# Banded attention and a four-expert FFN on one core: values two steps behind scores in the opening, other times for the weights

## The chip, the cores and the metric

The kernel runs on one core of a Trainium2 chip. What counts is the device time of one execution in microseconds. The kernel before takes 850.36 us in the median of three runs (849.62 to 850.9).

## The reference, cut to what matters

```python
def attn(q, k, v):                      # B=4, H=8, S=576, D=64
    s = (q @ k.transpose(0, 1, 3, 2)) / sqrt(64)
    rel = pos[:, None] - pos[None, :]
    plain = (rel >= 0) & (rel < 32)                      # heads 0 to 3
    dil = (rel >= 0) & (rel < 128) & (rel % 4 == 0)      # heads 4 to 7
    s = where(mask, s, -1e9); s = s - s.max(-1)
    a = exp(s); a = a / (a.sum(-1) + 1e-9)
    return a @ v
def moe(x, probs, w1, w2):              # N=2304, D=512, E=4, F=1024
    p = probs / (probs.sum(-1) + 1e-9)
    return sum(p[:, e] * (relu(x @ w1[e]) @ w2[e]) for e in range(4))
out = moe(attn(q, k, v) as rows of 512, probs, w1, w2)
```

## The kernel before, in words

**The attention** is cut into 48 groups: a batch, a pair of heads and a third of the sequence. They go in 25 steps (`steps`, L628): the first two hold one group each, the others two. The stages of a step are scores on TensorE (`s_qk`, tile sc, L271), six row maxima on VectorE that also put the masked scores into SBUF (`s_max`, L285), a subtraction on GpSimdE (`s_sub`, L301), the exponential on ScalarE (`s_exp`, L309), row sum and reciprocal on VectorE (`s_sum`, L317 and L318), the normalisation on GpSimdE (`s_norm`, L325), three transposes on TensorE and their copy by ScalarE (`s_tr`, tiles pt and pts, L336 and L340), and the product with the values on TensorE (`s_av`, tile po, L356), which ScalarE copies into xr (L372), the FFN's input. The tiles sc, pt and po take turns in four PSUM banks (pool pa).

**The loop** is at L713. In turn n it issues loads of q and k on SyncE's queue and of v on ScalarE's (for batches 0 and 1), and then the stages in the order of a table: the number beside a stage says how many steps it is behind. In before scores are at 0, transposes at 3, products at 4. The order in which the program issues is the order on each engine.

**The FFN** runs on expert blocks u of 256 columns and blocks of 576 rows of x. fp32 is done as three products of a high and a low part (names ending in h and l), and the first layer by Strassen-like sums (tiles m1x, m1y, hidden rows hh and hl), the second layer into m and the accumulator acc. The high part is a copy on ScalarE (L117), the low part a subtraction on VectorE or GpSimdE (L120). Pieces that split and sum weights and x are generators in a list `queue`: `step()` does one of them (a filler), and `need(...)` does all that stand ahead of one that is needed now. From turn START on (10 in before), the loop also takes two pieces of FFN a turn; `next(ffn)` may answer "idle". From OPEN on (15) it takes PACE of them a turn, until attention is done. Turns without FFN hold dummy matmuls (tile wt, L685) and fillers.

`fetch_w1` and `fetch_w2` load weights on SyncE's queue, `w1_split`, `w1_sums`, `w1_late` and `w2_late` are the pieces that prepare them; pw are the experts' shares, loaded in turn 4 (L740) and normalised by `weigh`. `done(groups)` says in which turn the last of some groups has had its product, from which START, OPEN and the times of the x pieces (`when`) follow.

Of the kernel before, what the change touches and what calls it, by code (L numbers as in the profile page):

```python
# [8 lines left out]
F32 = mybir.dt.float32  # L9
# [4 lines left out]
WINDOW = 32  # L14
# [4 lines left out]
GB = 6  # L19
GS = GB // 2  # L20
GW = GB * QB
PACE = 12


def band_masks(S):


    import numpy as np

    masks, which = [], []  # L30
    for run in (S, S // DILATION):
        for i in range(S // SB):
            a = (i * SB + np.arange(SB))[:, None]
            c = a // QB * QB - WINDOW + np.arange(KB)[None, :]
            seen = (c >= 0) & (a - c >= 0) & (a - c < WINDOW) & (a // run == c // run)
            m = np.where(seen, np.float32(0), np.float32(-8e9))
            same = [j for j, other in enumerate(masks) if np.array_equal(other, m)]
            if not same:
                same = [len(masks)]
                masks.append(m)  # L40
            which.append(same[0])
    return np.stack(masks), which
# [3 lines left out]
def kernel(  # L46
# [11 lines left out]
    nc = tc.nc  # L58
    _, which = band_masks(qT.shape[3])
    B, NP, _, S = qT.shape  # L60
    GP = S // GW
    NT, DM = out.shape
    E, _, F = w1.shape
# [18 lines left out]
    pw = const.tile([128, NTT, E], F32, name="pw")  # L82
# [16 lines left out]
    def fetch_w1(u):  # L99
        e, s = divmod(u % NU, FPE)  # L100
        r = wp.tile([128, 4, FU], F32, tag="r1", name="r1", bufs=2)
        nc.sync.dma_start(
            out=r, in_=w1[e, :, s * FU:(s + 1) * FU].rearrange("(c p) f -> p c f", p=128)
        )
        raw1[u] = r

    def fetch_w2(u):
        e, s = divmod(u % NU, FPE)
        r = wp.tile([128, 2, DM], F32, tag="r2", name="r2")
        nc.sync.dma_start(  # L110
            out=r, in_=w2[e, s * FU:(s + 1) * FU, :].rearrange("(c p) d -> p c d", p=128)
        )
        raw2[u] = r
# [110 lines left out]
    def attention(ap, xrp, pa):  # L224
# [18 lines left out]
            nc.gpsimd.memset(t[:, :, KB:], 1e-9)  # L243

        def load_qk(b, p, gi):
            q_s = ap.tile([128, GW], F32, tag="q", name="q_s", bufs=6)
            k_s = ap.tile([128, GW + WINDOW], F32, tag="k", name="k_s", bufs=6)
            nc.sync.dma_start(out=q_s, in_=qT[b, p][:, gi * GW:(gi + 1) * GW])
            nc.sync.dma_start(out=k_s, in_=kT[b, p][:, gi * GW:(gi + 1) * GW + WINDOW])
            qk_t[b, p, gi] = (q_s, k_s)  # L250
# [123 lines left out]
        def load_masks():  # L374
            nc.sync.dma_start(out=mask, in_=masks)


        stages = (
            (s_sub, 1), (s_sum, 2), (s_av, 4), (s_tr, 3), (s_norm, 2), (s_exp, 1),
            (s_qk, 0), (s_max, 0),  # L380
        )
        return chunk, load_masks, load_qk, load_v, stages


# [191 lines left out]
    def step(of=None):  # L576
        of = queue if of is None else of
        while of:
            if next(of[0][1], 0) != 0:
                return  # L580
            of.pop(0)

    def prepare(what, *args, soon=False, of=None):
        of = queue if of is None else of
        of.insert(0 if soon else len(of), ((what, args), what(*args)))
# [11 lines left out]
    with tc.manual_schedule():  # L597
# [11 lines left out]
        ap = early.enter_context(tc.tile_pool(name="attn", bufs=2, side="right"))  # L609
        xr_pool = xrp.__enter__()  # L610

        pools["chunk"], load_masks, load_qk, load_v, stages = attention(ap, xr_pool, pa)
        pairs = [(b, p) for b in range(B) for p in range(NP)]
        h0, h1 = range(NP // 2), range(NP // 2, NP)

        def batch(b, thirds):

            g = [(b, p, i) for p in h0 for i in range(GP)]
            return g + [(b, p, i) for part in thirds for p in h1 for i in part]
# [3 lines left out]
        first = batch(0, ((0, 2), (1,)))  # L623
# [2 lines left out]
            rest += batch(b, (range(GP),))  # L626
        rest = first + rest
        steps = [rest[:1], rest[1:2]] + [rest[i:i + 2] for i in range(2, len(rest), 2)]  # L628
        LAG = 4

        def done(*gs):

            return LAG + max(n for n, s in enumerate(steps) if any(g in s for g in gs))

        def begin():

# [17 lines left out]
        def weigh():  # L654

            nc.vector.reduce_sum(out=ps_, in_=pw, axis=mybir.AxisListType.X)
            nc.vector.tensor_scalar(
                out=ps_, in0=ps_, scalar1=1e-9, scalar2=None, op0=ALU.add
            )
            nc.vector.reciprocal(out=pr_, in_=ps_)  # L660
            nc.vector.tensor_tensor(
                out=pn, in0=pw, in1=pr_.to_broadcast([128, NTT, E]), op=ALU.mult
            )
# [17 lines left out]
        def dummies(n):  # L681

            for _ in range(n):
                wt = pools["m2"].tile([128, 512], F32, tag="m2", name="wt")
                nc.tensor.matmul(wt[:, :256], warm[:, :128], warm, start=True, stop=True)  # L685
# [5 lines left out]
        def dil(b, *thirds):  # L691
            return plains[b] + [(b, p, i) for p in h1 for i in thirds]


        START = done(*dil(0, 0, 2)) + 1
        OPEN = done(*dil(1, 0)) + 1
        when = {}
        for n, i, names in (
            (done(*plains[0]), 0, ("B11",)), (done(*plains[0]), 1, ("B11",)),
            (START - 1, 0, ("B21",)), (START - 1, 1, ("B21",)),  # L700
            (done(*dil(0, 1)), 0, ("X12", "B22", None, "t2", "t1", "t3")),
            (OPEN - 1, 1, ("X12", "B22", None)),
            (done(*dil(1, 1, 2)), 2, X_PARTS), (done(*dil(2, 0, 1)), 3, X_PARTS),
        ):
            when.setdefault(n, []).append((i, names))

        flat = [g for s in steps for g in s]
        first_x = []
        qk_done = qk_next = v_next = 0

        dummies(18)
        ffn = experts(begin)
        for n in range(len(steps) + LAG):  # L713
            while qk_next < min(qk_done + min(6, 3 + n), len(flat)):
                load_qk(*flat[qk_next])
                if qk_next == 0:
                    load_masks()
                qk_next += 1
            while v_next < len(steps) and v_next < max(n - LAG, 0) + 3 and v_next <= n:
                load_v(v_next, steps[v_next])  # L720
                v_next += 1
            for stage, lag in stages:
                if 0 <= n - lag < len(steps):
                    stage(n - lag, steps[n - lag])
            if n < len(steps):
                qk_done += len(steps[n])
            for i, names in when.get(n, ()):
                for name in names:
                    of = first_x if i < 2 else later
                    if name is None or name == "T2":  # L730
                        prepare(x_sums, i, of=of)
                    if name is not None:
                        prepare(x_part, i, name.upper(), of=of)
            queue[:0] = first_x
            first_x.clear()
            if n == 3:
                fetch_w1(0)
            if n == 4:
                fetch_w2(0)
                nc.sync.dma_start(out=pw, in_=probs.rearrange("(t p) e -> p t e", p=128))  # L740
            if n == 5:
                prepare(w1_split, 0)
            if n == 7:
                prepare(w2_late, 0)
                fetch_w1(1)
            if n == START + 1:
                weigh()
                prepare(w1_split, 1)
                prepare(w1_sums, 1)
            if n == OPEN - 1:  # L750
                prepare(w2_late, 1)
            if n == START + 2:
                fetch_w2(1)
            if n == OPEN:
                fetch_w1(2)
            if n == OPEN:
                gate.add("open")
            if n < START:
                dummies(4 if n < 4 else 1)
                step()  # L760
                if n > 4:
                    step()
                    step()
                continue
            for _ in range(PACE if "open" in gate else 2):
                if next(ffn) == "idle":
                    dummies(2)
                    for _ in range(3):
                        step()
                    break  # L770
                step()
                if len(queue) > 8:
                    step()
                elif later and len(queue) < 5:
                    step(later)
# [61 lines left out]
```

## Time and profile before

| | before |
|---|---|
| median of 3 runs | 850.36 us |
| profiled execution | 853.5 us, span 851.5 us |
| TensorE busy | 830.2 us, 97% of the span |
| VectorE, GpSimdE, ScalarE busy | 482.9, 404.5, 319.4 us |

```profile
PE   8798899999999999999999999999999999999998
DVE  4565755668656568755555545555555555455554
POOL 3456977777677668931431432332341341242210
PEclk8589999999999999999999999999999999999999
DMA  8872334223231122310100100100101001010003
```

Each digit is a fortieth of the span, 21.3 us; 9 is 90% or more busy. PEclk is TensorE's granted clock in tenths of full speed, which is 2.4 GHz; the other level is 1.2 GHz. The attention's opening is in the first three slices, and the second of them has the low clock. The chain of work that ended last is TensorE's for 90% of the span.

### The profile page before, as it was taken

What the parts mean: (1) busy time and instruction counts of PE and PEld (TensorE: products, weight loads), DVE (VectorE), ACT (ScalarE), POOL (GpSimd) and SP (SyncE); (2) the same over time, 40 slices, a digit from 0 to 9 for tenths busy, and PEclk for the clock granted to TensorE, in tenths of its full rate; (3) what the DMA queues carried; (4) which work ended last, traced back from release to release, by engine and by line L of the source; (5) the groups of instructions that cost most, each with busy time, mean ns of one, the idle gap of its engine ahead of it and who ended that gap; (6) DMA issues with size and microseconds to landing.
All of it is one profiled execution on the core that took longest, in us unless ns stands there. A gap on an engine that the chain in (4) does not pass through costs nothing.

```text
span 851.5 us, 15556 instructions
## 1 busy us (share of the span) xinstructions
PE 830.2 (97%) x6173; PEld 733.4 (86%) x6173; DVE 482.9 (57%) x1015; ACT 319.4 (38%) x761; POOL 404.5 (48%) x484
## 2 busy tenths in 40 slices
PE   8798899999999999999999999999999999999998
PEld 5577788888888888889899898898898998988986
DVE  4565755668656568755555545555555555455554
ACT  2344454545444444533333233232242242232321
POOL 3456977777677668931431432332341341242210
PEclk8589999999999999999999999999999999999999
DMA  8872334223231122310100100100101001010003
GB/s 233 217 197 77 122 112 122 89 90 118 83 102 61 50 75 75 124 49 26 50 26 25 50 25 26 50 26 27 49 25 50 26 26 50 25 34 17 1 25 123
DMA packets 51463, 59.16 MB, mean 69 GB/s; under 512 B 5952, under 2 KB 40896, under 8 KB 51392
## 3 DMA queue, kind: packets, MB, share of 16 engines
q1 hardware_dynamic: 47936, 53.46, 20.0%
q10 hardware_dynamic: 3456, 4.72, 2.2%
q8 instruction: 48, 0.79, 0.4%
q14 instruction: 23, 0.19, 0.1%
HBM read 53.45 MB, written 4.72 MB: 68 GB/s over the span
## 4 chain that ended last, share of the span: by engine, by line
PE 90%; DVE 3%; ACT 2%; DMA 2%; POOL 1%; issue 1%; ACTq 0%; POOLq 0%; DVEq 0%
PE m L487 45%; PE m1x L389 23%; PE m1y L389 17%; PE po L356 2%; PE sc L271 2%; DMA q_s<-qT 1%; PE pt L336 1%; PE wt L685 1%; DVE hl L413 1%; DMA v_s<-vw 1%; DVE acc L495 1%; DVE xl_T L120 1%; POOL g1l L120 0%; ACT hh L407 0%; DVE xr L207 0%
## 5 line engine op out<-in xcount | busy, mean ns | idle before, releaser
L495 DVE SCALAR_TENSOR_TENSOR acc<-m,pn,acc 128x512 f32<-128x512 f32 x270 | 201.8, 749 | 133.0 <-PE m L487 132.8
L487 PE MATMUL m<-w2h,hh 128*128 128x512 f32 x576 | 227.3, 395 | 3.6 <-DVE acc L495 3.1
L487 PE MATMUL m<-w2l,hh 128*128 128x512 f32 x576 | 226.0, 392 | 0.0
L120 POOL TENSOR_TENSOR g2l<-r,g2h 128x256 fp32r<-128x256 f32 x124 | 93.0, 777 | 240.7 <-PE m L487 212.2
L487 PE MATMUL m<-w2h,hl 128*128 128x512 f32 x576 | 179.1, 392 | 0.1
L407 ACT ACTIVATE hh<-s 128x384 fp32r<-128x384 f32 x94 | 49.4, 526 | 248.3 <-DVE s L430 197.8
L487 PEld LDWEIGHTS m<-w2h,hh 128*128 128x128 f32 x576 | 108.3, 188 | 26.2 <-DVE acc L495 5.7
L487 PEld LDWEIGHTS m<-w2h,hl 128*128 128x128 f32 x576 | 108.3, 188 | 24.3 <-DVE hl L413 0.6
L487 PEld LDWEIGHTS m<-w2l,hh 128*128 128x128 f32 x576 | 108.5, 188 | 20.1
L120 POOL TENSOR_TENSOR g1l<-r,g1h 128x256 fp32r<-128x256 f32 x93 | 69.1, 759 | 72.0 <-ACT g1h L117 72.0
L120 POOL TENSOR_TENSOR w2l<-r,w2h 128x512 fp32r<-128x512 f32 x62 | 80.5, 1317 | 45.4 <-ACT w2h L117 45.0
L446 DVE TENSOR_TENSOR s<-m1x,s 128x384 f32<-128x384 f32 x47 | 26.2, 558 | 103.2 <-PE m1x L389 101.7
L439 ACT ACTIVATE u<-m1x 128x384 f32<-128x384 f32 x47 | 23.1, 491 | 145.9 <-PE m1x L389 145.9
L413 DVE SCALAR_TENSOR_TENSOR hl<-s,hh 128x384 fp32r<-128x384 f32 x94 | 61.0, 648 | 28.8 <-ACT hh L407 28.8
L389 PE MATMUL m1x<-xh_T,g2h 128*128 128x384 f32 x156 | 52.9, 339 | 2.1 <-DVE s L430 1.8
L389 PE MATMUL m1x<-xl_T,g2h 128*128 128x384 f32 x156 | 52.5, 336 | 0.0
L389 PE MATMUL m1x<-xh_T,g2l 128*128 128x384 f32 x156 | 52.3, 335 | 0.0
L117 ACT ACTIVATE g2h<-r 128x256 fp32r<-128x256 f32 x125 | 43.4, 405 | 3.9 <-POOL r L149 3.9
L285 DVE CUSTOM_DVE_ANT_0 sm<-sc,mask 128x64 f32<-128x64 f32 x144 | 23.0, 222 | 36.8 <-PE sc L271 36.1
L389 PE MATMUL m1y<-xl_B,g2h 128*128 128x384 f32 x128 | 43.4, 339 | 0.0
L389 PE MATMUL m1y<-xh_B,g2h 128*128 128x384 f32 x128 | 43.4, 339 | 0.0
L389 PE MATMUL m1y<-xh_B,g2l 128*128 128x384 f32 x128 | 43.3, 338 | 0.0
(91 smaller groups left out, 1507.6 us busy)
## 6 DMA issues: line engine op xcount, KB each, us to landing
r<-w SPq DMA_DIRECT2D x64, 512.0 KB, 3.4
k_s<-kT SPq DMA_DIRECT2D x48, 112.0 KB, 3.5
v_s<-vw ACTq DMA_DIRECT2D x24, 192.0 KB, 4.5
q_s<-qT SPq DMA_DIRECT2D x48, 96.0 KB, 3.9
v_s<-vw SPq DMA_DIRECT2D x24, 192.0 KB, 3.8
out<-acc SPq DMA_DIRECT2D x18, 256.0 KB, 2.0
mask<-masks SPq DMA_DIRECT2D x1, 192.0 KB, 4.1
pw<-probs SPq DMA_DIRECT2D x1, 36.0 KB
```

What stands on the lines that cost most here:

```text
L117: nc.scalar.activation(out=hi, in_=src, func=AF.Copy)
L120: lo_eng.tensor_tensor(out=lo, in0=src, in1=hi.bitcast(F32), op=ALU.subtract)
L271: nc.tensor.matmul(banks[swap][o:o + QB, i * KB:(i + 1) * KB], q_s[h, c0:c0 + QB], k_s[h, c0:c0 + KB], start=True, stop=True, skip_group_c ...
L285: nc.vector.tensor_tensor_reduce(out=sm[:, i * len(gs) + k, :KB], in0=banks[k][:, i * KB:(i + 1) * KB], in1=mask[:, which[blk if p < NP // ...
L356: nc.tensor.matmul(po[k][64 * j:64 * j + 64, o:o + QB], v_s[rows, j, 2 * i + half, :], ts_[rows, c:c + QB], start=True, stop=True,)
L389: nc.tensor.matmul(bank, w[:, k], x[:, k], start=(first and k == 0 and i == 0), stop=(last and k == 1 and i == 2), skip_group_check=True,)
L407: nc.scalar.activation(out=hi, in_=src, func=AF.Relu)
L413: nc.vector.scalar_tensor_tensor(out=lo, in0=src, scalar=0.0, in1=hi.bitcast(F32), op0=ALU.max, op1=ALU.subtract)
L439: nc.scalar.activation(out=u2, in_=x, func=AF.Copy)
L446: nc.vector.tensor_tensor(out=s5, in0=x, in1=s5, op=ALU.add)
L487: nc.tensor.matmul(po, h, w, start=(n == 0 and x == 0), stop=(n == 3))
L495: nc.vector.scalar_tensor_tensor(out=acc, in0=po, scalar=pn[:, tt, e:e + 1], in1=acc, op0=ALU.mult, op1=ALU.add,)
```

## The change

Steps 0 to 10 (those up to the group `(1, NP - 1, 0)`, `opening` in number) get a table of their own, `first`: products two steps behind scores, transposes one, and another order of issue. With `done` it moves START from 10 to 8 and OPEN from 15 to 13. Turn numbers of loads and splits are now told from START: first weights in turn 4 (3 before), w2 in turn 6 (4), `w1_split(0)` in turn 6 (5), `w2_late(0)` in turn 8 (7), the second weights and `weigh` in turn 7 (7 and 11), their split and sums in turn 9 (11). pw is the very first transfer, on ScalarE's queue. At most four groups of q and k are loaded ahead, in four buffers each. Turns ahead of START hold four fillers and two dummies (four in the first three turns); a turn that is idle four fillers. PACE is 10.

```diff
-PACE = 12
+PACE = 10
...
-            q_s = ap.tile([128, GW], F32, tag="q", name="q_s", bufs=6)
-            k_s = ap.tile([128, GW + WINDOW], F32, tag="k", name="k_s", bufs=6)
+            q_s = ap.tile([128, GW], F32, tag="q", name="q_s", bufs=4)
+            k_s = ap.tile([128, GW + WINDOW], F32, tag="k", name="k_s", bufs=4)
...
-        stages = (
+        first = (
+            (s_sum, 1), (s_norm, 1), (s_av, 2), (s_qk, 0), (s_max, 0), (s_tr, 1),
+            (s_sub, 0), (s_exp, 0),
+        )
+        then = (
             (s_sub, 1), (s_sum, 2), (s_av, 4), (s_tr, 3), (s_norm, 2), (s_exp, 1),
             (s_qk, 0), (s_max, 0),
         )
+        stages = (first, then)
...
-        LAG = 4
+        AHEAD = 4
+        opening = [n for n, s in enumerate(steps) if (1, NP - 1, 0) in s][0] + 1
+
+        def lag(n):
+
+            return 2 if n < opening else 4
 
         def done(*gs):
 
-            return LAG + max(n for n, s in enumerate(steps) if any(g in s for g in gs))
+            return max(n + lag(n) for n, s in enumerate(steps) if any(g in s for g in gs))
...
+        nc.scalar.dma_start(out=pw, in_=probs.rearrange("(t p) e -> p t e", p=128))
         dummies(18)
         ffn = experts(begin)
-        for n in range(len(steps) + LAG):
-            while qk_next < min(qk_done + min(6, 3 + n), len(flat)):
+        for n in range(len(steps) + 4):
+            while qk_next < min(qk_done + AHEAD, len(flat)):
...
-            while v_next < len(steps) and v_next < max(n - LAG, 0) + 3 and v_next <= n:
+            while v_next < len(steps) and v_next + lag(v_next) <= n + 2:
                 load_v(v_next, steps[v_next])
                 v_next += 1
-            for stage, lag in stages:
-                if 0 <= n - lag < len(steps):
-                    stage(n - lag, steps[n - lag])
+            for late, order in enumerate(stages):
+                for stage, after in order:
+                    if 0 <= n - after < len(steps) and late == (n - after >= opening):
+                        stage(n - after, steps[n - after])
...
-            if n == 3:
+            if n == START - 4:
                 fetch_w1(0)
-            if n == 4:
+            if n == START - 2:
                 fetch_w2(0)
-                nc.sync.dma_start(out=pw, in_=probs.rearrange("(t p) e -> p t e", p=128))
-            if n == 5:
                 prepare(w1_split, 0)
-            if n == 7:
+            if n == START - 1:
+                fetch_w1(1)
+                weigh()
+            if n == START:
                 prepare(w2_late, 0)
-                fetch_w1(1)
             if n == START + 1:
-                weigh()
                 prepare(w1_split, 1)
                 prepare(w1_sums, 1)
+            if n == START + 2:
+                fetch_w2(1)
             if n == OPEN - 1:
                 prepare(w2_late, 1)
-            if n == START + 2:
-                fetch_w2(1)
...
             if n < START:
-                dummies(4 if n < 4 else 1)
-                step()
-                if n > 4:
-                    step()
+                dummies(4 if n < 3 else 2)
+                for _ in range(4):
                     step()
                 continue
             for _ in range(PACE if "open" in gate else 2):
                 if next(ffn) == "idle":
                     dummies(2)
-                    for _ in range(3):
+                    for _ in range(4):
                         step()
```

The order on TensorE just ahead of the first expert product, before (po is the product with values, pt the transposes, sc the scores, wt a dummy, m1x the first FFN product):

```order
L356 MATMUL po<-pts,v_s 64x32 x24
L336 MATMUL pt<-ident,pb 128x128 x3
L271 MATMUL sc<-k_s,q_s 32x64 x24
L685 LDWEIGHTS ident
L685 MATMUL wt<-ident 128x256
L356 MATMUL po<-pts,v_s 64x32 x24
L336 MATMUL pt<-ident,pb 128x128 x3
L271 MATMUL sc<-k_s,q_s 32x64 x24
L389 MATMUL m1x<-xh_B_0_681,g1h 128x384
```

And the same place in the changed kernel:

```order
L695 LDWEIGHTS ident
L695 MATMUL wt<-ident 128x256
L695 LDWEIGHTS ident
L695 MATMUL wt<-ident 128x256
L356 MATMUL po<-pts,v_s 64x32 x24
L271 MATMUL sc<-k_s,q_s 32x64 x24
L336 MATMUL pt<-ident,pb 128x128 x3
L394 MATMUL m1x<-xh_B_0_563,g1h 128x384
```

The transposes have moved behind the scores, and there they belong to the step before these scores and not to the one three steps back; two dummies stand between them and the next product.

The order on ScalarE in the turn in which before splits the first half of w2(0), several turns ahead of its product (xr the copy out of PSUM, sm the exponential, xh_B an x part):

```order
L372 ACTIVATE xr<-po 128x4x48 x2
L340 ACTIVATE pts<-pt 128x384
L309 ACTIVATE sm_94<-sm_94 128x6x64
L117 ACTIVATE xh_B_0_681<-xr 128x2x192 x2
L117 ACTIVATE w2h<-r_412 128x512
```

And in the changed kernel the turn that splits it, which is the turn of its first product:

```order
L372 ACTIVATE xr<-po 128x4x48 x2
L340 ACTIVATE pts<-pt 128x384
L309 ACTIVATE sm_95<-sm_95 128x6x64
L117 ACTIVATE xh_T_0_1082<-xr 128x2x192
L117 ACTIVATE xh_T_0_1086<-xr 128x2x192
L117 ACTIVATE xh_T_0_1090<-xr 128x2x192
L117 ACTIVATE w2h<-r_655 128x512 x2
L117 ACTIVATE g1h<-r_759 128x256 x3
```

Three x parts (xh_T) and this turn's exponential stand ahead of both halves of w2h, and the split of the second w1 (g1h) follows in the same turn.

## Rows read from the trace of the kernel before

**Rows 1.** Busy time by stretch: us; PE, PEld, DVE, ACT, POOL; PEclk; DMA; GB/s
```profile
14.03:44.23 30.20, 23.78 (x620) 17.82 (x619) 15.47 (x92) 11.76 (x34) 12.92 (x15) 0.50 0.90 227
44.23:68.52 24.29, 22.47 (x547) 17.88 (x542) 16.32 (x85) 11.25 (x31) 12.79 (x15) 0.92 0.73 189
68.52:105.91 37.39, 32.14 (x237) 27.75 (x233) 25.02 (x58) 16.56 (x42) 30.46 (x33) 0.91 0.30 90
105.91:200.00 94.09, 93.59 (x994) 81.75 (x993) 58.30 (x154) 44.53 (x111) 68.52 (x82) 1.00 0.36 112
```
**Rows 2.** Timeline of TensorE: start, us, instruction, [idle before and its releaser]
```profile
9.45 0.52 PE L336 MATMUL pt<-ident,pb 128*64 128x128 f32 x3
...
21.83 0.43 PE L271 MATMUL sc<-k_s,q_s 64*32 64x64 f32 x4
27.14 0.93 PE L271 MATMUL sc<-k_s,q_s 64*32 64x64 f32 x44 [4.88 <-ACT xr L372]
...
28.33 1.51 PE L356 MATMUL po<-pts,v_s 64*64 64x32 f32 x48
29.77 0.90 PE L336 MATMUL pt<-ident,pb 128*128 128x128 f32 x3
30.60 0.97 PE L271 MATMUL sc<-k_s,q_s 64*32 64x64 f32 x48
...
31.82 1.51 PE L356 MATMUL po<-pts,v_s 64*64 64x32 f32 x48
...
44.23 0.69 PE L389 MATMUL m1x<-xh_B,g1h 128*128 128x384 f32 x1
```
**Rows 3.** Timeline of ScalarE around the hole
```profile
26.75 0.55 ACT L372 ACTIVATE xr<-po 128x192 f32<-128x192 f32 x2 [7.31 <-DMA q_s<-qT]
```
**Rows 4.** Timeline of SyncE's queue
```profile
18.19 4.51 SPq L248 DMA_DIRECT2D q_s<-qT  x1
```
**Rows 5.** Bytes moved from 14 to 30 us, in 40 slices of 0.4 us
```profile
GB/s 216 291 330 336 362 291 310 304 261 265 270 229 264 214 261 249 178 144 117 92 71 108 152 146 196 202 141 49 61 223 188 218 139 248 236 284 328 300 294 239
```
**Rows 6.** Groups of lines, 14 to 44.2: busy, mean ns | idle before, releaser
```profile
L301 POOL TENSOR_TENSOR sm<-sm,nm 128x384 f32<-128x384 f32 x6 | 6.0, 1003 | 11.0 <-DVE nm L285 11.0
...
L325 POOL TENSOR_TENSOR pb<-sm,rc 128x384 f32<-128x384 f32 x7 | 5.8, 826 | 3.4 <-DVE rc L318 3.2 <-ACT xr L372 0.2
L285 DVE CUSTOM_DVE_ANT_0 sm<-sc,mask 128x64 f32<-128x64 f32 x36 | 5.8, 221 | 14.0 <-PE sc L271 14.0
L317 DVE TENSOR_REDUCE su<-sm 128x6 f32<-128x390 f32 x6 | 3.3, 549 | 0.0
L309 ACT ACTIVATE sm<-sm 128x384 f32<-128x384 f32 x6 | 3.2, 530 | 0.0
...
L340 ACT ACTIVATE pts<-pt 128x384 f32<-128x384 f32 x6 | 3.0, 495 | 0.3 <-PE pt L336 0.3
L120 DVE TENSOR_TENSOR w2l<-r,w2h 128x512 fp32r<-128x512 f32 x2 | 2.0, 996 | 0.0
...
L117 ACT ACTIVATE xh_B<-xr 128x384 fp32r<-128x384 f32 x4 | 1.9, 522 | 0.0
...
L117 ACT ACTIVATE w2h<-r 128x512 fp32r<-128x512 f32 x2 | 1.3, 628 | 0.0
L318 DVE RECIPROCAL rc<-su 128x6 f32<-128x6 f32 x6 | 1.2, 192 | 0.2
```
**Rows 7.** Timeline of TensorE: attention on the full clock
```profile
48.30 0.90 PE L356 MATMUL po<-pts,v_s 64*64 64x32 f32 x48
49.14 0.55 PE L336 MATMUL pt<-ident,pb 128*128 128x128 f32 x3
49.61 0.72 PE L271 MATMUL sc<-k_s,q_s 64*32 64x64 f32 x48
```
**Rows 8.** Timeline of TensorE: two holes behind the opening
```profile
83.44 0.41 PE L389 MATMUL m1x<-xh_T,g2h 128*128 128x384 f32 x1 [1.83 <-DVE s L430]
...
103.18 0.79 PE L487 MATMUL m<-w2h,hh 128*128 128x512 f32 x1 [2.56 <-DVE acc L495]
```

## The prediction

> **What bounds the kernel now.** I read first the busy times by stretch [rows 1]. From 105.91 on, TensorE works 93.59 of 94.09 us: there the kernel is bound by TensorE alone, and no rearrangement gains anything. What the change can move lies ahead of that, in three stretches. From 14.03 to 44.23 only attention runs, on a granted clock of 0.50, TensorE busy for 23.78 of 30.20 us. From 44.23 (first expert matmul, [rows 2]) to 68.52 attention loops hold a few expert products each; 22.47 of 24.29 us are busy. From 68.52 to 105.91 the expert products run freely, and still 5.25 of 37.39 us are idle and the clock is 0.91.
>
> Next I read TensorE's timeline. One opening loop on the half clock is product, transpose, scores and a dummy, 28.33 to 31.82: 3.49 us [rows 2]. One hole stands out: scores that begin at 21.83 go on at 27.14, after 4.88 us idle, released by ScalarE's copy out of PSUM [rows 2]. That copy had waited 7.31 us for a q load [rows 3]; SyncE needed 4.51 us to issue that load, right behind the shares pw [rows 4]. The row of bytes moved shows what pw does to the transfers: from some 300 GB/s at the start to 141 in the mean of the ten slices from 20.4 to 24.4 us [rows 5].
>
> Last, the softmax chain, from the groups of lines in the same stretch [rows 6]: six row maxima of 0.22, subtraction 1.00, exponential 0.53, row sum 0.55, reciprocal 0.19, normalisation 0.83. Most of the 1.33 us of maxima lies behind the last score matmul, so with hand-offs I count 4.7 us from the end of a step's scores to its transpose.
>
> **The change part by part.** TensorE has the same 3627 rows in its program and the same 44 dummies before and after. So the time moves only by its idle time and by what runs on the half clock, and I sum by stage.
>
> *To the first expert matmul.* Before: 10 loops, and 44.23, of it 4.88 us for the pw hole. After: 8 loops, since values come two steps behind scores. Each loop then holds, on the half clock, a transpose (0.83), the wait for its copy by ScalarE (0.50 [rows 6] and hand-offs, 0.71; the two dummies fill it), a product (1.44) and scores (0.97), by the distances between starts and the durations in [rows 2]; and a wait that before does not have: the next transpose takes the PSUM bank of the first half of this step's scores, which VectorE's maxima read last. Its price by [rows 6]: between 0.2 (one maximum) and 1.33 (all six); I take 0.96, five of them less the part beside the second half of the scores. Sum 0.83 + 0.71 + 1.44 + 0.97 + 0.96 = 4.9 us, and the chain of 4.7 just fits into it. So a loop costs 4.9 instead of 3.49. The first transpose stands at 9.45 [rows 2] and stays there; the scores of step 2 end about 2.5 us later, at 12, and the transpose that belongs to them begins 4.7 later, at 16.7. Five more loops of 4.9 bring that of step 7 to 41.2. The fillers (four a loop instead of three) put weight and x splits on VectorE ahead of the row sum in three of these loops: splits of about w2l's 1.00 us [rows 6], of which I count 0.7 each as late, since VectorE has gaps: 43.3; with its 0.83 it ends at 44.1. So the first expert matmul stays at about 44.2, as before: two loops fewer and the hole gone (2 x 3.49 + 4.88 = 11.9), paid back by eight longer loops. Where this could end otherwise: if the bank wait is 0.2, seven loops give 5 us less; if the chain is late behind fillers by a whole 1.0 a loop, 2 more.
>
> *From there to the opening (OPEN).* Before 24.29 us. After, the same expert work, with these holes: loop 8 the bank wait, 1.0; loop 9 the same wait with VectorE also computing the first hidden rows and x splits, 2.0 (bounds 1.0 and 3.0); loop 10 the weights. Before, w2h(0) is split at step 7, long ahead of its use; after, the split is queued at START and is done only when the products ask for it, behind exponential, three x splits of 0.52 and itself 0.63 on ScalarE and 1.00 on VectorE [rows 6]. TensorE has done its transpose by then: from the end of the scores 0.96 + 1.00 + 0.53 + 1.56 + 0.63 and hand-offs, 4.9, less the bank wait and a transpose at full clock (0.96 and 0.47), about 3.2 us, and 0.8 more for the second half of w2l. Loads two steps ahead instead of three add about 0.8. Sum of holes 1.0 + 2.0 + 3.2 + 0.8 + 0.8 = 7.8; 1.8 us of idle time in before go off it. As loops 11 to 13 change over from two steps behind to four, one product and two transposes fall out of this stretch, on the full clock 0.84 and twice 0.47 [rows 7]: 1.8. So it lasts 24.3 + 7.8 - 1.8 - 1.8 = 28.5 and OPEN comes at 72.7, 4.2 later. Those 1.8 us are then still owed, and the scores of two steps as well (8 loops instead of 10), 2 x 0.72 [rows 7]: 3.2. At OPEN after is 4.2 + 3.2 = 7.4 us behind.
>
> *From OPEN to 106.* Before loses 5.25 us there by idling, 1.83 and 2.56 in single holes [rows 8], and 0.09 x 37.39 = 3.4 by the clock: 8.6. The holes come from GpSimdE, busy for 30.46 of 37.39 us, and from VectorE behind it. After, the splits and sums of the second weights (L120 and L145 to L151) are done at loops 9 to 11, ahead of OPEN, and the x sums of the third block come three loops later. I give back the 2.56, half of 1.83, and half of the clock's 3.4: 5.2, bounds 2 and 7.5. That leaves 7.4 - 5.2 = +2.2.
>
> *Priced at nothing:* PACE 10 instead of 12 only spreads attention over more products; TensorE stays fed, its cover is the queue of expert products (93.59 of 94.09 us). Four instead of six q and k buffers: loads still leave two steps ahead, some 9 us, against the 4.51 of the slowest issue seen. Weighing the shares earlier lies in VectorE's idle time (15.47 of 30.20 busy). pw first on ScalarE's queue: from 0, if its packets fall where nothing waits, to (300 - 141)/300 x 4 = 2.1 us late for the first loads; I take 0, since the first scores there follow 18 dummies. The Trainium skill ("DMA: Bandwidth & Descriptors", section "Issuing engines are not separate DMA queues") says that transfers from any engine's queue share the same sixteen engines and interleave, so the queue would save only the issue. [Rows 5] agree that pw slows all transfers; by that rule the price moves to the start rather than going, and the sum would be up to 2.1 higher.
>
> The sum is made on the profiled execution: 853.5 + 2.2 = 855.7. The profiled execution lies 3.1 over the median of 850.36, so the forecast on the median's scale is 850.36 + 2.2, about 852.5.
>
> **The rivals.** *B, faster:* the opening runs at the pace of the chain with little bank wait and fewer late fillers. Then START comes 5 us earlier, of which the later holes take none back: 852.5 - 5 = 847.5; with the rest of GpSimdE's give-back (7.5 instead of 5.2), 845.2. For it: the hole of 4.88 surely goes and 2 loops fall away. Against it: 0.50 of the clock with 23.78 of 30.20 busy says that TensorE's own work, not the chain, fills most of a loop.
>
> *C, slower:* the clock. In before it is back at full soon after the first expert products, 0.92 over that stretch [rows 1]. After has a hole in each of loops 8, 9 and 10, the last of 3 to 4 us. If the half clock lasts until loop 11, the products of those loops (some 22.47 / 24.29 of 12 us) take twice as long on about 5 us of work: 852.5 + 5 = 857.5, and 3 more with the give-back's lower bound, 860.7. It decides from the point where loop 9's m1 products read 0.69, the half-clock value [rows 2], and not half of that. The row that bears on it is the clock of 0.50 up to 44.23, with TensorE busy 79% of the time [rows 1]. The Trainium skill ("TensorE: Matmul & The Clock Gate", section "A second HAM failure mode: psum-queue depth-cycling") tells of a kernel whose clock swung between both levels as it waited on PSUM banks each turn; by that rule C would come true. The trace agrees so far as the opening of before, with its waits, is at 1.2 GHz.
>
> *D, no change:* the hole was hidden, since what is late at 27 us is caught up where before idles later, and the sum of all is within a microsecond of before: 849.5 to 851.5. For it speaks that the terms above come to 2.2 from pieces of 12, 8 and 5; against it, that each of them would have to be off in one direction.
>
> **How the numbers follow.** My forecast (848 to 856, the likeliest at 852.5) gets 0.50, B 0.27, C 0.16, D 0.07. A measurement of this kernel can tell 0.2%, 1.7 us, from no change. B is all faster; of my forecast 0.05 is faster, 0.20 the same, 0.25 slower; D is the same; C slower. That gives faster 0.32, same 0.27, slower 0.41. The range leaves out the last bounds of B and C: 845.5 to 857.5.
>
> **What would show it right or wrong.** Right: in the profile of the changed kernel the hole at 21.83 is gone; opening loops measure 4.7 to 5.1 us; transposes wait for VectorE's maxima about 1 us each; the first m1x stands at 43 to 46; a hole of 3 us or more ahead of the first product with w2h (loop 10), released by w2h or w2l; OPEN at 71 to 74; and under 3 us idle from OPEN to 106. Wrong: a first m1x before 41 (B), the clock under 0.85 from there to OPEN (C), holes behind OPEN as long as before, or loads of q and k that TensorE waits for now that fewer are ahead. A first transpose later than 9.45 by a microsecond or more would show the price of pw.

## The result and the profile after

The changed kernel takes 861.75 us in the median (861.0 to 862.22), before 850.63 beside it: ratio on record 1.0121, 95% interval 1.0105 to 1.0137 (the two medians alone would give 1.0131). Slower by 11.1 us between the medians, where 852.5 was forecast and 845.5 to 857.5 was the range. The span of the profiled execution is 860.4 us against 851.5; TensorE's busy time is the same, 830.0 and 830.2. So the 8.9 us between the spans are idle time in sum. That hides the half clock, which lengthens busy time: what it adds in the second stretch below (24.75 us busy, 22.47 before) is about what the shorter first one saves (21.39, 23.78 before).

Busy time of the changed kernel by stretch, columns as in [rows 1]; the bounds are the first expert matmul, the first one behind OPEN, and the expert matmuls that stand in before at 105.91, 200 and 300:

```profile
14.03:43.01 28.98, 21.39 (x580) 16.92 (x579) 14.58 (x94) 11.11 (x30) 11.67 (x15) 0.50 0.86 231
43.01:76.74 33.73, 24.75 (x489) 19.11 (x488) 15.19 (x67) 11.53 (x30) 16.78 (x20) 0.72 0.33 93
76.74:109.95 33.21, 30.28 (x284) 26.25 (x283) 22.05 (x70) 16.08 (x39) 22.63 (x27) 1.00 0.43 131
109.95:203.98 94.03, 93.18 (x993) 81.24 (x993) 59.27 (x154) 45.20 (x112) 72.65 (x85) 1.00 0.37 111
203.98:308.75 104.77, 102.02 (x947) 89.09 (x947) 65.75 (x131) 49.39 (x124) 71.26 (x83) 1.00 0.27 87
```

And the last stretch in before:

```profile
200.00:300.00 100.00, 99.50 (x848) 87.38 (x847) 61.61 (x115) 47.39 (x117) 70.13 (x81) 1.00 0.24 77
```

Against [rows 1] the stretches differ by -1.2, +9.4, -4.2, -0.1 and +4.8 us, 8.7 in sum. In the second, TensorE idles 8.98 us (1.82 before) and its clock is 0.72 (0.92). In the last, 2.75 us are idle (0.50 before), and 2.5 more are busy time, 102.02 against 99.50: attention that was still owed (144 score matmuls there against 96, 336 products with values against 288).

TensorE's timeline after, in the opening, columns as in [rows 2]:

```profile
9.07 0.52 PE L336 MATMUL pt<-ident,pb 128*64 128x128 f32 x3 [1.42 <-POOL pb L325]
...
21.29 0.87 PE L336 MATMUL pt<-ident,pb 128*128 128x128 f32 x3 [0.67 <-DVE nm L285]
...
25.88 0.87 PE L336 MATMUL pt<-ident,pb 128*128 128x128 f32 x3 [0.67 <-DVE nm L285]
...
31.44 0.90 PE L336 MATMUL pt<-ident,pb 128*128 128x128 f32 x3 [1.65 <-POOL pb L325]
...
36.87 0.90 PE L336 MATMUL pt<-ident,pb 128*128 128x128 f32 x3 [1.54 <-POOL pb L325]
...
42.46 0.90 PE L336 MATMUL pt<-ident,pb 128*128 128x128 f32 x3 [1.65 <-POOL pb L325]
...
55.67 0.90 PE L336 MATMUL pt<-ident,pb 128*128 128x128 f32 x3 [2.49 <-POOL pb L325]
59.38 0.80 PE L492 MATMUL m<-w2h,hh 128*128 128x512 f32 x1 [2.81 <-ACT w2h L117]
60.62 0.79 PE L492 MATMUL m<-w2l,hh 128*128 128x512 f32 x1 [0.45 <-DVE w2l L120]
...
68.41 0.72 PE L336 MATMUL pt<-ident,pb 128*128 128x128 f32 x3 [1.74 <-POOL pb L325]
...
214.71 0.50 PE L492 MATMUL m<-w2h,hh 128*128 128x512 f32 x1 [0.93 <-DVE acc L500]
221.14 0.50 PE L492 MATMUL m<-w2h,hh 128*128 128x512 f32 x1 [0.94 <-DVE acc L500]
229.77 0.45 PE L394 MATMUL m1x<-xh_T,g1h 128*128 128x384 f32 x1 [0.62 <-DVE s L451]
```

The hole of 4.88 us [rows 2] is gone. In its place nearly every transpose waits: 0.67 us for the maxima that free its PSUM bank, from 31 us on mostly 1.5 to 2.5 us for the normalisation. The w2 products of turn 10 start behind 2.49 and 2.81 us of idling, and 0.80 us long: the half clock, while the m1 products at 50 us had been at the full one. The last three rows are a loss where the prediction had priced PACE at nothing, since TensorE "stays fed".

VectorE ahead of the first hole of turn 10 (hl is the low part of hidden rows, xr the x sums):

```profile
51.97 0.56 DVE L418 SCALAR_TENSOR_TENSOR hl<-m1x,hh 128x384 fp32r<-128x384 f32 x1 [1.88 <-ACT hh L412]
52.44 0.55 DVE L207 TENSOR_TENSOR xr<-xr 128x384 f32<-128x384 f32 x1
52.91 0.55 DVE L418 SCALAR_TENSOR_TENSOR hl<-m1y,hh 128x384 fp32r<-128x384 f32 x1
53.38 0.55 DVE L207 TENSOR_TENSOR xr<-xr 128x384 f32<-128x384 f32 x1
```

And the chain of waits through the two holes (start, us, what; su is the row sum):

```profile
53.92 0.48 DVE su L317
...
54.79 0.83 POOL pb L325
...
55.67 0.92 PE pt L336 x3
...
56.67 0.49 ACT pts L340
57.16 0.41 ACT sm L309
57.57 1.23 ACT xh_T L117 x3
58.80 0.53 ACT w2h L117
...
59.35 2.63 DVE w2l L120 x2
```

Both are read from the top: the row sum of step 9 stands on VectorE behind two hidden rows and two x sums, the transpose waits for it, and the split of w2 waits on ScalarE behind that transpose's copy, the exponential and three x splits, as the prediction had it.

### The profile page after: what moved, and what is told of

Same layout as the page of the kernel before. It is cut to its first block, busy times and chain, and to the rows that moved or that the text cites. A ratio compares the mean times of both kernels' runs of the same rounds, so it can differ in the third digit from the quotient of the medians.

```text
span 860.4 us, 15531 instructions
## 1 busy us (share of the span) xinstructions
PE 830.0 (96%) x6173; PEld 733.4 (85%) x6173; DVE 481.9 (56%) x1015; ACT 320.1 (37%) x761; POOL 402.5 (47%) x484
## 4 chain that ended last, share of the span: by engine, by line
PE 89%; DVE 4%; POOL 3%; ACT 2%; issue 1%; DMA 1%; ACTq 0%; POOLq 0%; DVEq 0%
PE m L492 44%; PE m1x L394 23%; PE m1y L394 17%; PE po L356 2%; PE pt L336 1%; PE sc L271 1%; DMA v_s<-vw 1%; DVE xl_B L120 1%; PE wt L695 1%; POOL pb L325 1%; POOL g1l L120 1%; DVE hl L418 0%; DVE acc L500 0%; POOL sm L301 0%; ACT hh L412 0%
## 5 line engine op out<-in xcount | busy, mean ns | idle before, releaser
L418 DVE SCALAR_TENSOR_TENSOR hl<-s,hh 128x384 fp32r<-128x384 f32 x94 | 58.9, 626 | 28.0 <-ACT hh L412 27.8
L117 ACT ACTIVATE w2h<-r 128x512 fp32r<-128x512 f32 x64 | 38.3, 621 | 0.0
```

Source lines behind the costliest of these rows:

```text
L117: nc.scalar.activation(out=hi, in_=src, func=AF.Copy)
L418: nc.vector.scalar_tensor_tensor(out=lo, in0=src, scalar=0.0, in1=hi.bitcast(F32), op0=ALU.max, op1=ALU.subtract)
```

## The experiments

Two theories compete in the texts on record below. L: two steps behind scores put the whole softmax chain, and every split queued in its engines, on TensorE's path. W: the late split of w2(0) is most of the loss. P and P2 are about the late rows at 214 to 230 alone: whether PACE, or the x parts queued there, make them.

Times are medians in us; the ratio is to before in runs beside it. Before itself was not the same in each set of runs, so runs of different sets are compared by the ratio.

| run | what it is | time | before beside it | ratio, 95% interval |
|---|---|---|---|---|
| | changed kernel | 861.75 | 850.63 | 1.0121 (1.0105 to 1.0137) |
| e1 | changed, w2(0) split early | 858.56 | 851.69 | 1.0082 (1.0062 to 1.0102) |
| e2 | changed, four behind | 853.75 | 851.69 | 1.0025 (1.0008 to 1.0041) |
| e5 | before, pw first | 850.33 | 851.69 | 0.9987 (0.9969 to 1.0004) |
| e6 | e1 and e2, six buffers | 851.45 | 852.24 | 0.9992 (0.9977 to 1.0007) |
| e7 | before, two behind, PACE 10 | 863.16 | 852.24 | 1.0138 (1.0118 to 1.0159) |
| e8 | e1, second w1 split late | 860.90 | 852.24 | 1.0109 (1.0085 to 1.0133) |
| e9 | changed, x parts later | 861.40 | 852.24 | 1.0113 (1.0094 to 1.0132) |
| e10 | changed, three behind | 855.42 | 851.29 | 1.0047 (1.0028 to 1.0066) |
| e11 | e1, three behind, six buffers | 854.50 | 851.29 | 1.0032 (1.0014 to 1.0051) |
| e12 | changed, START 10, OPEN 15 | 861.28 | 851.29 | 1.0111 (1.0083 to 1.0140) |
| e13 | changed, holes filled | 859.18 | 852.96 | 1.0085 (1.0063 to 1.0106) |
| e14 | changed, OPEN 14 | 862.51 | 851.55 | 1.0134 (1.0109 to 1.0158) |
| e15 | changed, PACE 11 | 869.06 | 851.55 | 1.0206 (1.0182 to 1.0231) |

**Which part of the change it is: e2 and e7.** All steps four behind, the rest as changed (START and OPEN go back to 10 and 15 with it):

```diff
-            return 2 if n < opening else 4
+            return 4
-        stages = (first, then)
+        stages = (then, then)
```

> The changed kernel with all steps four behind and the old order of stages; START and OPEN go back to 10 and 15, and the turns of the weights go with them (w2_late(0) still only at START). Rival L: the waits of transposes for GpSimdE's normalisation (1.5 to 2.5 us in each of turns 6 to 11) are gone, time 851 to 854. Theory W: the exponential ahead of the w2 split is ready earlier, but the split is still asked for by its own product, so a hole of 1.5 to 3 us and some half clock stay: 855 to 859.

853.75: 8 of the 11 us are gone, by L's number. W's mechanism is there too; TensorE's timeline at turn 12:

```profile
60.13 0.64 PE L492 MATMUL m<-w2h,hh 128*128 128x512 f32 x1 [3.98 <-ACT w2h L117]
```

The opposite edit, in before: the table `first`, `lag(n)` with the v loads' bound that goes by it, and PACE 10, and nothing else of the change.

> The kernel before with only the order of the opening changed: two steps behind in steps 0 to 10, START 8 and OPEN 13 follow, PACE 10; six buffers, weights fetched in turns 3 and 4 and split in turns 5 and 7, pw on SyncE's queue in turn 4. Theory L: the transposes wait for the normalisation in turns 6 to 11 as in the changed kernel, and most of the loss is there: 856 to 860. Theory W: with the weights at their old turns most of the loss goes: 850 to 854. If two steps behind and later weights both cost only together (fillers of four a turn on the chain), 850 to 853 too, but then no transpose waits over 1 us.

863.16: the opening's table alone, with PACE 10, costs all that the whole change costs. (PACE 10 without that table costs nothing that can be measured: e6 below.) The table holds two things, the distances and another order of issue, and no run tells these apart: e10 changes both. The transposes of e7 wait as in the changed kernel, and the second half of w2(0) is late as well, behind the same three x splits:

```profile
56.47 0.55 PE L336 MATMUL pt<-ident,pb 128*128 128x128 f32 x3 [2.49 <-POOL pb L325]
59.88 0.79 PE L492 MATMUL m<-w2h,hh 128*128 128x512 f32 x1 [2.41 <-ACT w2h L117]
```

**The late w2: e1, e6 and e8.** e1 fetches w2(0) with w1(0) and splits it a turn earlier:

```diff
             if n == START - 4:
                 fetch_w1(0)
+                fetch_w2(0)
             if n == START - 2:
-                fetch_w2(0)
                 prepare(w1_split, 0)
             if n == START - 1:
+                prepare(w2_late, 0)
...
-            if n == START:
-                prepare(w2_late, 0)
```

> The changed kernel with w2(0) fetched in turn 4 and its split queued in turn 7, as far ahead of its first product as in before; all else as changed. Theory W (most of the loss is the late w2 split: the holes of 2.81, 0.45 and 0.19 us ahead of and in the first w2 products, and the half clock that lasts from there to 72 us): the holes go, the clock is full from 47 us to the opening at OPEN, OPEN moves from 75 to 68 to 70, time 854 to 857 (861.75 before this edit). Rival L (two steps behind scores: each transpose waits for its softmax chain, and a filler put earlier makes a chain later): the hole moves to a transpose in turns 7 to 10, OPEN stays within 2 us of 75, time 859.5 to 862.

858.56, between the two. The hole ahead of the w2 product goes and part of it is back at the next transposes, since GpSimdE's splits of x and w1 stand ahead of their normalisation. TensorE's timeline, then GpSimdE's:

```profile
57.85 0.55 PE L336 MATMUL pt<-ident,pb 128*128 128x128 f32 x3 [2.49 <-POOL pb L325]
65.76 0.90 PE L336 MATMUL pt<-ident,pb 128*128 128x128 f32 x3 [3.76 <-POOL pb L325]
```

```profile
59.95 2.93 POOL L120 TENSOR_TENSOR xl_T<-xr,xh_T 128x384 fp32r<-128x384 f32 x3 [1.05 <-ACT xh_T L117]
62.82 2.10 POOL L120 TENSOR_TENSOR g1l<-r,g1h 128x256 fp32r<-128x256 f32 x3
64.86 0.84 POOL L325 TENSOR_TENSOR pb<-sm,rc 128x384 f32<-128x384 f32 x1
```

e6 takes e1's edit, four behind, and six q and k buffers with loads six ahead:

> The changed kernel with all steps four behind (START 10, OPEN 15), with w2(0) fetched at START-4 and split from START-1, and with six q and k buffers and loads up to six groups ahead. What is left of the change is the later weights, pw first on ScalarE's queue, the fillers and PACE 10. Theory W plus L (the two causes are separate and their prices add): no hole ahead of the first w2 product (3.98 us with four behind alone), no wait of 3.30 us for k_s at 13 us, time 848 to 851. Rival (the two repair the same loss, so that the second brings nothing): 852.5 to 854.5, as with four behind alone (853.75).

851.45, no difference from before that can be measured. What is left of the change in e6 (pw, later weights, fillers, PACE 10) brings nothing and costs nothing. Against e2 it gains 0.3%; early w2 and buffers were not told apart there.

e8 is e1 with `prepare(w1_split, 1)` and `w1_sums` at START + 3 instead of START + 1:

> The changed kernel with w2(0) early (858.56 alone) and the split and sums of the second w1 queued in turn 11 instead of 9. If the waits of 2.49 and 3.76 us of the transposes in turns 10 and 11 come from the splits on GpSimdE ahead of the normalisation (three xl_T and three g1l), the second of them falls to under 2 us and OPEN comes 1 to 2.5 us earlier; what is not done there is done behind OPEN, where GpSimdE is the late one, so the time is 856 to 858.5. Rival (the softmax chain itself is too long for one step, whatever is queued): both waits stay over 2 us, 858 to 860.

The second wait falls from 3.76 to 1.74 us, as expected of splits ahead of it; the time does not fall with it: 860.90, above both ranges that were expected, with an interval that overlaps e1's.

**The clock: e13.** Dummies in the holes of turns 10 and 11:

```diff
+                        if stage.__name__ == "s_tr":
+                            dummies({START + 2: 14, START + 3: 10}.get(n, 0))
...
+            if n == START + 2:
+                dummies(18)
```

> The changed kernel with dummy matmuls in its holes: 14 ahead of turn 10's transposes, 18 behind them, 10 ahead of turn 11's; nothing is waited for that was not before. It tells the price of the holes from that of the clock that falls behind them (in the changed kernel 0.72 from the first expert matmul to OPEN). If rival C of the prediction holds (the clock's fall costs about 4 us on top of the holes): the clock from there to OPEN is over 0.85, m2 products of turn 10 take 0.40 and not 0.63 us, OPEN comes 3 to 4.5 us earlier than 76.7, time 857 to 859. If the holes alone cost (other engines set the pace of turns 10 to 12 at either clock): OPEN within 1.5 us of 76.7, time 860.5 to 862.5.

Timeline of e13, and its stretch from the first expert matmul to OPEN:

```profile
58.90 0.50 PE L492 MATMUL m<-w2h,hh 128*128 128x512 f32 x1
...
73.20 0.44 PE L394 MATMUL m1x<-xh_T,g1h 128*128 128x384 f32 x1
```

```profile
43.54:73.20 29.66, 27.00 (x532) 19.86 (x530) 14.96 (x67) 11.59 (x30) 16.58 (x20) 0.94 0.40 106
```

The clock stays full through turns 10 and 11 (0.94 in the stretch, whose first 3 us are still at half), OPEN comes at 73.20 instead of 76.74, and the profiled span is 857.1 instead of 860.4. So the clock's fall behind the holes cost about 3.5 us at OPEN (3.3 between the spans). That it is no matter of the one profiled execution shows in the granted clock of all: 0.970 to 0.972 in the four of the changed kernel, 0.974 to 0.982 in the six of e13. The waits themselves, now full of dummies, and the late loss are still paid.

**How many steps behind: e10, e11, e12.** Three behind, the transpose two:

```diff
-            (s_sum, 1), (s_norm, 1), (s_av, 2), (s_qk, 0), (s_max, 0), (s_tr, 1),
+            (s_sum, 1), (s_norm, 1), (s_av, 3), (s_tr, 2), (s_qk, 0), (s_max, 0),
-            return 2 if n < opening else 4
+            return 3 if n < opening else 4
```

> The changed kernel with the opening's transposes two steps behind scores and its products three (START 9, OPEN 14); all else as changed, w2(0) late as well. Theory L (the loss is that a transpose one step behind has the whole softmax chain, and every split queued in it, on TensorE's path): transposes wait under 0.5 us in the opening turns, the hole ahead of the first w2 product stays at 2 to 4 us as with four behind, time 851.5 to 855. Rival (FFN work that starts before turn 10 meets splits that are not done, whatever the distance between scores and transposes): the loss halves only, 856 to 859.

> Three behind as in the run beside it, with w2(0) early and six q and k buffers: what may beat both kernels. Theory L plus W: no hole over 1.5 us from 15 to 75 us, a first expert matmul at 38 to 42, time 846 to 850. Rival: what comes earlier is given back behind OPEN by GpSimdE, so 850 to 852.5, as with four behind (851.45).

855.42, just over L's upper bound, and 854.50, above both ranges expected of e11: no version that beats before. In e10 no transpose of turns 3 to 12 waits for a normalisation (the first one, in turn 2, waits 1.12 us); the w2 hole stays (4.09 us), and scores wait instead, 3.60 us once for a v load and up to 1.84 us for ScalarE's copies. In e11 the w2 hole is gone, and its worst row is at the change to four behind:

```profile
69.33 0.90 PE L336 MATMUL pt<-ident,pb 128*128 128x128 f32 x3 [4.05 <-POOL pb L325]
```

e12 adds 2 to START and OPEN, two behind kept.

> The changed kernel with START and OPEN put back to turns 10 and 15, two steps behind kept. If the loss is in the expert products that stand among opening turns whose transposes are late (L in its narrow form), these products now stand in turns with four behind: the holes of 2 to 3 us go, but two more opening turns of 5 us come first; against before 10 x (5.0 - 4.4) = 6 us, so 856 to 859. If START two turns earlier is the whole cause, 850 to 853. If the opening's length is all (10 turns at 5.2 and more): 861 to 864.

861.28: an earlier START is not the cause; ten opening turns with late transposes (2.68 us at 46.24, 2.74 at 52.86) cost as much as eight and the products among them.

**pw: e5.** Before, with pw's load first on ScalarE's queue.

> The kernel before with only the load of the shares moved: first transfer, on ScalarE's queue. If the hole of 4.88 us at 22 to 27 is pw's doing and on the path: no hole, first expert matmul at 39.5 to 40, time 846 to 848 (850.5 before). Rival D: the time is given back later (weights not there, GpSimdE late), so 849.5 to 851.5. Rival: the first loads come late behind pw, scores start at 6.5 or later, 851 to 853.

850.33, no gain that can be measured, and the first expert matmul stands at 44.16 (44.23 before). The hole stays without pw, 3.58 us. Timelines of TensorE and ScalarE in e5:

```profile
14.74 0.89 PE L356 MATMUL po<-pts,v_s 64*64 64x32 f32 x24 [1.96 <-ACT pts L340]
...
27.42 0.94 PE L271 MATMUL sc<-k_s,q_s 64*32 64x64 f32 x44 [3.58 <-ACT xr L372]
```

```profile
10.41 3.49 ACTq L256 DMA_DIRECT2D v_s<-vw  x2
...
24.14 2.85 ACTq L256 DMA_DIRECT2D v_s<-vw  x2
```

And the same two places in before, TensorE's first product with values and ScalarE's issue ahead of the copy at 26.75 [rows 3]:

```profile
11.27 0.89 PE L356 MATMUL po<-pts,v_s 64*64 64x32 f32 x24
```

```profile
20.69 6.01 ACTq L256 DMA_DIRECT2D v_s<-vw  x2
```

In both kernels ScalarE issues two v loads right ahead of the copy that ends the hole (27.04 in e5), for 2.85 us in e5 and 6.01 in before. What is shorter there is paid at the start, where pw now falls: the first product stands at 14.74 instead of 11.27. So pw is not what makes the hole. What does stays open. With the weights fetched later it is gone in e2 (no wait over 1 us from 14 to 43, though one of 3.30 at 12.97 for a k load), but in e6, which fetches w1(0) and w2(0) later too, in one turn, TensorE waits 3.00 us at 35.30 for a copy of the same kind. Which of the weight loads it takes was not tried.

**The late loss and PACE: e3, e9, e14, e15.** e3 is the changed kernel with PACE 12.

> The changed kernel with PACE 12. Theory P (about 3 of the lost us are lost between 205 and 240, where VectorE has the x parts of a later block, softmax and accumulators together, and PACE decides that they meet there): the holes of 0.93, 0.94 and 0.62 us there go, time 858.5 to 859.5. Rival: they come from where the opening left the queue of splits, and stay; time 861 to 862.5.

863.72. With PACE 12 the FFN comes to the sums of the last x rows before these are queued, so this kernel leaves out the wait for them; its time says little. e15, PACE 11, has all waits:

> The changed kernel with PACE 11, all else as changed. Phase: the turns of attention stand elsewhere against the FFN's blocks, the holes at 214, 221 and 229 go or move, idle from 204 to 309 changes by over 1 us either way: 859 to 863. If PACE 10 itself (fewer FFN pieces a turn) is no part of it: idle there stays at 2.5 to 3 us and the time at 861 to 862.5.

869.06, 7 us slower than with PACE 10. TensorE's and VectorE's timelines:

```profile
351.02 0.69 PE L394 MATMUL m1x<-xh_T,g1h 128*128 128x384 f32 x1 [7.67 <-DVE s L451]
```

```profile
340.44 8.08 DVE L207 TENSOR_TENSOR xr<-xr 128x384 f32<-128x384 f32 x8
```

The FFN asks for the last x sums when attention has only just made their rows: eight sums in one piece on VectorE, TensorE waiting. With OPEN two turns earlier, a PACE of 12 or 11 outruns attention; that is what PACE 10 buys.

e9 queues the x parts of chunk 3 one turn later (`done(*dil(2, 0, 1)) + 1`), e14 has OPEN one turn later.

> The changed kernel with the x parts of chunk 3, which VectorE splits, queued one turn later. Theory P2 (2.5 to 3.5 of the lost us are lost at 205 to 240, where those parts stand on VectorE between a step's softmax and the accumulators): the holes of 0.93, 0.94 and 0.62 us there go, time 858.5 to 859.5. Rival: they only move by a turn, 861 to 862.5.

> The changed kernel with OPEN one turn later (14); START and two steps behind kept. In every trace so far with OPEN 13 TensorE idles some 2.3 us more between 204 and 309 us than in before, waiting for accumulators (L500) and sums (L451) of VectorE; in none with OPEN 14 or 15. If this late loss hangs on where the turns of attention stand against the FFN's blocks (phase): the holes at 214, 221 and 229 are gone, idle there under 1 us, and one idle turn more at OPEN is paid with under 1.5 us: 859 to 861. If it comes from the two steps behind themselves: holes and time stay, 861 to 863.

e9: two of the three holes go, others come at 233 and 238 (0.85 and 0.83 us); 861.40, not told apart from the changed kernel. e14, the stretch of the late loss:

```profile
204.00:309.00 105.00, 104.22 (x871) 91.52 (x870) 65.44 (x120) 48.77 (x122) 72.79 (x86) 1.00 0.26 81
```

0.78 us idle instead of 2.75, so the late loss hangs on where attention's turns stand against the FFN's blocks and not on the two steps (e12, two behind with OPEN 15, idles 0.53 us from 204 to 309). The time is no better, 862.51, and the span about the same (860.1): what is gained there is lost ahead of it, more than the 1.5 us that I allowed.

## Why the prediction was wrong

The step that failed is the stretch from the first expert matmul to OPEN, where the sum kept the clock of before behind holes that it had itself forecast. Two more terms were off, PACE at nothing and the loss given back behind OPEN. In the prediction's terms: 2.2 us were forecast; OPEN came 4.0 later than the sum, 1.0 less was given back, 2.25 us of idling came late, and 0.7 less attention was owed (2.5 instead of 3.2). That makes 8.7 of the 8.9 us between the spans. Point by point, by its own steps:

- *First expert matmul at 44.2, with the hole gone and eight longer loops:* 43.01. A loop is 4.59 us (21.29 to 25.88) and 5.4 to 5.6 with fillers in the chain, forecast 4.9 and 0.7 more in three; the bank wait is 0.67, forecast 0.96. Right.
- *Holes of 7.8 us up to OPEN:* 8.98, with the w2 hole where it was placed; turn 9 has none (forecast 2.0), turns 10 and 11 have 2.49 and 1.74 at transposes. Near in sum, in part by luck: the wait put to loop 8 falls ahead of this stretch (1.65 at 42.46), and the 0.8 for loads two steps ahead did not show (no load is waited for here), the w2 term of 3.2 and 0.8 measured 2.81 and 0.64, and 1.26 us in front of OPEN's first matmul were not in it. The 3.2 is also a slip: 4.9 less 0.96 and 0.47 is 3.5.
- *OPEN at 72.7:* 76.74. Here the sum failed. It carried the clock of before, 0.92, into a stretch with such holes; measured is 0.72. The stretch is 33.73 us long, forecast 28.5: 1.2 of the difference is idle time, 4.0 is matmuls that took longer. That is rival C, by its mark in the profile (under 0.85) and in the main by its price: 3.5 us by e13, 5 forecast. The clock fell a turn later than C's point, though: turn 9's m1 products are at full clock, turn 10's w2 products at half. With the clock kept, e13's OPEN is 73.20, 0.5 from the forecast. I put the holes in the sum and the clock's answer to them in a rival of 0.16, though both follow from the same rows.
- *5.2 us given back behind OPEN:* that stretch got 4.2 shorter, idle 2.93 instead of 5.25 us and the clock full. But 3.4 us of what I let before lose there is half clock, half of it behind the hole of 2.56 at 103.18 [rows 8]. e5, the same program there, has a smaller hole and the full clock (0.50 instead of 0.79 us):

```profile
101.18 0.50 PE L487 MATMUL m<-w2h,hh 128*128 128x512 f32 x1 [1.75 <-DVE acc L495]
```

  e5's span is 3.4 us shorter with no measurable gain in time. So some of the loss was most likely of the one profiled execution, which lay 3.1 us over its median; a credit against it is none against the median. The other executions on record bear this out: of the 85 of before that ran beside the experiments, the 15 with a granted clock of 0.975 or less (the profiled one had 0.975) took 854.4 us in the median, the 35 with 0.979 or more 851.3. It is also most of why 8.9 us between spans are 11.1 between medians.
- *PACE priced at nothing, "TensorE stays fed":* 2.25 us more idle from 204 to 309 us. e14 shows that they hang on the phase, e15 that one more piece a turn costs 7 us. Setting PACE to 10 was not what lost them: with PACE 10 and OPEN 15, e2 idles 0.50 us there.
- *pw:* the first transpose stands at 9.07, not later than 9.45, but it comes one step behind instead of three, so the sign says little. The first scores start at 5.32 and 7.08 as in before, so the changed kernel pays nothing there. e5 does, 3.5 us at its first product, and gains nothing in all. The reading that ScalarE's copy waited for a q load was also wrong: its queue was issuing two v loads for 6.01 us, and the copy, which the row puts down to a q load, reads no q. That pw's price moves to the start in e5 fits the Trainium skill ("DMA: Bandwidth & Descriptors", section "Issuing engines are not separate DMA queues"): another queue changes who issues, not what the transfers share.
- *Rival B:* its condition failed; the first expert matmul came 1.2 us earlier, not 5.

The rule that C cites from the Trainium skill ("TensorE: Matmul & The Clock Gate", section "A second HAM failure mode: psum-queue depth-cycling") agrees with this trace in that waits between groups of matmuls brought the half clock. But the wait ahead of the fall was for other engines' splits and normalisations, not for PSUM banks.

The cause, then: the opening's table, two steps behind with the transposes one behind, puts the whole softmax chain and every split queued in it on TensorE's path (e2, e7). Part of its price is the clock that falls in the holes (e13). 2.25 us of idling come from a phase of the FFN in which TensorE waits for VectorE, and taking that phase away gave no time back (e14). What stays open is why they come from just this phase, how distance and order share the loss, and how the rest divides between chain and w2: e1 takes 3 us off, not all.

## What to carry to other kernels

A shorter pipeline saves turns only while its longest chain, with everything that is queued into that chain's engines, still fits in one turn: sum the chain with the fillers in it. Where a sum forecasts a new hole of some microseconds on TensorE, put the half clock behind it into the same sum, at the least as a price with a high chance. Before crediting a removed loss, check that it belongs to the kernel and not to the one execution that was profiled, above all where that lies over its median.

## What had not been expected of the hardware

Dummy matmuls in holes kept the clock at its full level through 5.3 us in which nothing else was ready, and 3.5 us came back (e13). Without them it fell ahead of the transposes at 55.67 (0.90 us long instead of 0.55), and the w2 products behind ran 0.63 to 0.80 us instead of 0.39 to 0.50 until 72 us, although TensorE was busy for most of that time. The length of the hole alone does not decide it: behind a wait of the same 2.49 us the transposes of e1 (57.85) and e7 (56.47) still took 0.55 us, and the clock was at half only behind their next hole (65.76 in e1, 59.88 in e7).
